# FFN gate and up computed as rows, with x stationary and the weights moving in four column groups, in a one-core decode kernel

## The chip, the cores and the metric

The kernel runs on one core of one Trainium2 chip. The metric is device time in microseconds (us), lower is better. Every time below is a median over executions of one program; the span in a profile is that of one profiled execution, some 1.5 us less than the device time. A change counts as faster or slower from 2% on. Experiments of one batch ran on one chip and share the runs of the kernel before.

Names: PE is TensorE (matmuls), PEld its weight loads, DVE is VectorE, ACT is ScalarE, SP is the engine whose queue issues the transfers. "K tile n" is the n-th of 32 tiles of the key cache, 8.4 MB each.

## The reference, cut to what matters

One decode step, batch 1, one token, D = 448. Part A is attention with 16 query heads over a cache of 8 heads x 65,536 positions x 256; part B is a small FFN; a gate mixes them. All inputs are bf16.

```python
gate = jnp.einsum("bsd,df->bsf", x, W_gate)      # W_gate, W_up: [448, 1792]
up   = jnp.einsum("bsd,df->bsf", x, W_up)
gate = gate * (gate > 0)
b    = jnp.einsum("bsf,fd->bsd", gate * up, W_down)
...
return g * a + (1 - g) * b                       # a: attention over the cache
```

The caches are 2 x 268.4 MB. The two FFN matrices that the change touches are 1.6 MB each.

## The kernel before

Three ring slots of 64 KB per partition take turns in holding tiles of K and V. At the start, slot 2 holds the weights of q, gate, up and down; K tile 0 goes to slot 0, K tile 1 to slot 1, and K tile 2 must wait until slot 2 is free. All these transfers are issued in order on one queue (SP). DVE transposes every K tile in eight pieces, PE multiplies it with q (QK), DVE takes the maximum, ACT the exponential.

The gate/up stage, before. F is 1792, R3 is 3, FT is 14. The *weights* are stationary, 128 columns at a time, and x moves, one column. So h comes out with its features on partitions, as the down projection wants it, but every matmul yields one column:

```python
def f_gu(e):
    for ft in range(FT):
        for which in range(2):                       # gate, up
            c = which * 14 + ft
            for kt in range(R3):
                e.matmul(GU_ps[:, c:c + 1], wf3[which][:, kt * F + ft:(kt + 1) * F:FT], xT[:, kt:kt + 1],
                         start=(kt == 0), stop=False, skip_group_check=True)
            for half in range(2):                    # the last 64 rows of D
                ins = e.matmul(GU_ps[64 * half:64 * half + 64, c:c + 1], wfh[which][:, ft:F // 2:FT],
                               xT[:, R3 + half:R3 + half + 1], start=False, stop=True, skip_group_check=True)
    return ins
```

An operation carries a key, and each engine runs its operations in the order of their keys. These keys matter here (`tk` and `tg` are planned landing times, 31.05 and 38.75):

```python
tr = [op("dv", tk + 2.22 * w, f_trans(sl, w), [kd]) for w in range(8)]   # transposes of a K tile
l_["relu"] = mop("dv", tg + 12, ...)                                     # 50.75: behind the transposes of K tile 0
l_["hT"]   = mop("dv", tg + 12.1, ...)
l_["dn"]   = op("pe", tg + 12.2, f_dn, [l_["hT"], a3])                   # 28 down matmuls; then slot 2 is free
qk[n, b]   = op("pe", tk + (9 * (b + 1) if n else 20 + b), ...)          # QK of tile 0 stands behind them
...
kd = dma("sp", t, "r%d" % sl, ..., free(("k", n)))                       # K tile 2: waits for gu and dn
```

Of the kernel before, what the change touches and what calls it, by code (L numbers as in the profile page):

```python
# [7 lines left out]
F32 = mybir.dt.float32  # L8
# [4 lines left out]
ALU = AluOpType  # L13
# [11 lines left out]
class _Plan:  # L25
# [8 lines left out]
    def op(self, eng, key, fn, deps=()):  # L34
        o = _Op(eng, key, fn, deps)
        self.ops.append(o)
        return o
# [82 lines left out]
def bass_gated_mix__gqa_block_cached__glu_gated_reglu__decode_kernel(  # L120
# [17 lines left out]
    F = B_W_gate.shape[1]  # L138
# [6 lines left out]
    R3 = D // 128  # L145
    NR3 = R3 * 128
    NX = R3 + 2
    FT = F // 128
# [7 lines left out]
    with es:  # L156
        sb = lambda name, shape, dt: es.enter_context(nc.sbuf_tensor(name, shape, dt))
# [3 lines left out]
        P_sb = sb("P_sb", [128, 2048], BF)  # L161
# [5 lines left out]
        identf = sb("identf", [128, 128], F32)  # L167
# [4 lines left out]
        xT = sb("xT", [128, NX], BF)  # L172
        gz = sb("gz", [1, 4], F32)
        gb = sb("gb", [128, 2], F32)
# [7 lines left out]
        X = sb("hs", [128, 20], F32)  # L182
        attnT = sb("attnT", [128, H * 4], BF)
        hT = sb("hT", [128, FT], BF)
        gtmp2 = sb("gtmp2", [128, FT], F32)


        xw = P_sb[:, 0:NX * 160]
        iot = P_sb[:, 800:1056].bitcast(I32)
        qn = P_sb[:, 1056:1568]  # L190
        x_row = P_sb[0:1, 2048 - D:2048]
        fin_o = P_sb[0:1, 0:D]
        gw_row = scr[0:1, 0:D]
# [7 lines left out]
        wf3 = [ring[2][:, WB + i * R3 * F:WB + (i + 1) * R3 * F] for i in range(2)]  # L201
        WB += 2 * R3 * F
        wfh = [ring[2][:, WB + i * (F // 2):WB + (i + 1) * (F // 2)] for i in range(2)]
# [5 lines left out]
        OP = ps("O", [128, 512], F32)  # L209
        A_ps = ps("A_ps", [128, 512], F32)  # L210
        M_ps = ps("M_ps", [128, 512], F32)
        QN_ps = ps("QN", [128, 512], F32)[:]
        VT_ps = M_ps[0:2, 0:128]
        NMR_ps = M_ps[:, 128:129]
        GU_ps = M_ps[:, 448:476]
        T_ps = M_ps[:, 480:484]
        GB_ps = M_ps[:, 496:498]
        LS_ps = M_ps[:, 500:502]
# [3 lines left out]
        op, dma = pl.op, pl.dma  # L222
        touch_m = []

        def mop(*a, **k):
            o = op(*a, **k)
            touch_m.append(o)
            return o
# [57 lines left out]
        c_ps = []  # L286
# [5 lines left out]
        g_idf = op("gp", 0.2, lambda e: e.tensor_scalar(identf[:], iot, 0.0, None, ALU.is_equal), [g_idb])  # L292
# [22 lines left out]
        z7 = mop("dv", 1.7, lambda e: e.tensor_copy(gb[:], GB_ps), [z6])  # L315
# [13 lines left out]
        x2_ = mop("dv", 0.7, lambda e: e.tensor_copy(xT[:], XT_ps), [x1_])  # L329
# [64 lines left out]
        l_, qk, smax, aexp, pv, last = {}, {}, {}, {}, {}, {}  # L394
# [55 lines left out]
        for kind, i, t in issue:  # L450
# [10 lines left out]
            elif kind == "gu":  # L461
                a1 = []
                for i_, W in enumerate((B_W_gate, B_W_up)):
# [2 lines left out]
                    a1.append(dma("sp", t + 0.01 * i_ + 0.005, "wfh%d" % i_, lambda e, W=W, i_=i_: e.dma_start(  # L466
                        wfh[i_], W[NR3:D, :].rearrange("r (t f) -> (r t) f", t=2))))

                def f_gu(e):
                    for ft in range(FT):  # L470
                        for which in range(2):
                            c = which * 14 + ft
                            for kt in range(R3):
                                e.matmul(GU_ps[:, c:c + 1], wf3[which][:, kt * F + ft:(kt + 1) * F:FT], xT[:, kt:kt + 1],  # L474
                                         start=(kt == 0), stop=False, skip_group_check=True)
                            for half in range(2):
                                ins = e.matmul(GU_ps[64 * half:64 * half + 64, c:c + 1], wfh[which][:, ft:F // 2:FT],  # L477
                                               xT[:, R3 + half:R3 + half + 1], start=False, stop=True, skip_group_check=True)
                    return ins
                tg = tL["gu", 0]  # L480
                l_["gu"] = mop("pe", tg, f_gu, a1 + [x2_])
                l_["relu"] = mop("dv", tg + 12, lambda e: e.tensor_scalar_max(gtmp2[:], GU_ps[:, 0:FT], 0.0), [l_["gu"]])
                l_["hT"] = mop("dv", tg + 12.1, lambda e: e.scalar_tensor_tensor(
                    hT[:], gtmp2[:], gb[:, 1:2], GU_ps[:, 14:14 + FT], ALU.mult, ALU.mult), [l_["relu"], z7])
            elif kind == "wd":
                a3 = dma("sp", t, "wd", lambda e: e.dma_start(wd_sb, B_W_down.rearrange("(p ft) d -> p ft d", ft=FT)), [l_["q"]])

# [6 lines left out]
            elif kind == "k":  # L494
                n = i
                h, t_ = divmod(n, NTH)
# [116 lines left out]
        pe = progs["pe"]  # L613
# [54 lines left out]
```

## Time and profile before

The kernel before takes 1277.39 us (6 runs, 1277.16 to 1277.75).

| | before |
|---|---|
| span of the profiled run | 1275.5 us |
| bytes read | 549.03 MB, 430 GB/s |
| busy PE / DVE / ACT | 33% / 50% / 5% |
| gate/up matmuls | 39.1 to 52.6 us |
| K tile 2 issued | 55.94 us |
| transposes of K tile 1 start | 63.22 us |

From the page of the kernel before: busy time by engine; the span in 40 equal slices, as tenths that the DMA engines were busy and as GB/s; the total.

```profile
PE 423.9 (33%) x4652; PEld 169.6 (13%) x4652; DVE 635.1 (50%) x428; ACT 63.4 (5%) x124; POOL 4.3 (0%) x21
...
DMA  9999999999999999999999999999999999999998
GB/s 402 447 427 428 434 434 442 432 430 432 436 436 436 430 432 432 434 438 436 427 432 438 436 432 434 432 432 432 438 438 427 432 436 436 434 434 432 419 442 351
...
HBM read 549.03 MB, written 0.00 MB: 430 GB/s over the span
...
L368 DVE STREAM_TRANSPOSE ring<-ring 128x2048 uint32<-128x2048 uint32 x256 | 565.4, 2275 | 395.2 <-DMA ring<-in_A_k_cache_dram 395.2
```

The last line says that DVE sat idle for 395.2 us before its transposes, waiting for DMA. No compute engine is near full. DMA is at its highest digit in every slice but the last and moves 419 to 447 GB/s in all but the first and the last.

The stage, from the timeline of the kernel before. Columns: start in us, duration in us (of a merged run of instructions, from the first start to the last end), engine, source line, operation, output<-inputs, shapes, count; in brackets the idle time before it and what ended that.

```profile
31.13 17.66 DVE L368 STREAM_TRANSPOSE ring<-ring 128x2048 uint32<-128x2048 uint32 x8 [7.77 <-DMA ring<-in_A_k_cache_dram]
39.11 0.31 PE L474 MATMUL M_ps<-xT,ring 128*128 128x1 bf16 x3 [17.58 <-DMA ring<-in_B_W_up_dram]
39.35 0.28 PE L477 MATMUL M_ps<-xT,ring 128*64 128x1 bf16 x2
...
52.64 0.17 DVE L482 TENSOR_SCALAR gtmp<-M_ps 128x14 f32<-128x14 f32 x1 [3.85 <-PE M_ps L477]
52.85 0.23 DVE L483 SCALAR_TENSOR_TENSOR hT<-gtmp,gb,M_ps 128x14 bf16<-128x14 f32 x1
53.13 2.40 PE L390 MATMUL A_ps<-ring,hT 128*1 128x224 bf16 x24 [0.53 <-DVE hT L483]
...
55.54 4.07 PE L379 MATMUL ST<-ring,xc 128*16 128x512 bf16 x62
55.94 4.05 SPq L498 DMA_DIRECT2D ring<-in_A_k_cache_dram  x2
...
63.22 2.31 DVE L368 STREAM_TRANSPOSE ring<-ring 128x2048 uint32<-128x2048 uint32 x1 [2.86 <-DMA ring<-in_A_k_cache_dram]
```

The last weights land at 39.1, PE works through the 140 matmuls, DVE makes hT, PE does the down matmuls, and at 55.94 the queue may issue K tile 2. At that moment K tile 1 is still on its way: DVE waits for it until 63.22. So the queue holds work when K tile 2 joins it. DVE spends 31.1 to 48.8 us in the transposes of K tile 0.

### The profile page before, as it was taken

The page shows a single profiled execution, that of the slowest core. Times are in us where ns is not written, and L with a number is a line of the kernel's source. Part 1 is how long each engine was busy: PE and PEld are TensorE (multiplying, and loading weights), DVE is VectorE, ACT ScalarE, POOL GpSimd, SP SyncE. Part 2 cuts the span into 40 slices and gives each one's busy share as a digit, 9 for nine tenths or more (in the row PEclk, how much of TensorE's full clock was granted, in tenths as well). Part 3 has the DMA queues.
Part 4 walks back from the last instruction along what each step waited for, and adds up shares of the span by engine and source line. Part 5 has one row for each costly group of instructions (what it writes and reads, how often), then busy time and mean ns, then how long its engine had stood idle before and what let it go on. Part 6 is the DMA issues. An engine that isn't in the chain of part 4 may idle for free. (4 is left out here: it accounts for less than half of the span.)

```text
span 1275.5 us, 10391 instructions
## 1 busy us (share of the span) xinstructions
PE 423.9 (33%) x4652; PEld 169.6 (13%) x4652; DVE 635.1 (50%) x428; ACT 63.4 (5%) x124; POOL 4.3 (0%) x21
## 2 busy tenths in 40 slices
PE   3633322334123532224331343321333314233235
PEld 1501110111001210011110111110111101011012
DVE  2597633465533655434555444555435655336600
ACT  0001000010000100001000010000100001000000
POOL 1000000000000000000000000000000000000000
PEclk8656666656666575667656666656666656666567
DMA  9999999999999999999999999999999999999998
GB/s 402 447 427 428 434 434 442 432 430 432 436 436 436 430 432 432 434 438 436 427 432 438 436 432 434 432 432 432 438 438 427 432 436 436 434 434 432 419 442 351
DMA packets 12052, 549.22 MB, mean 431 GB/s; under 512 B 1283, under 2 KB 1798, under 8 KB 3078
## 3 DMA queue, kind: packets, MB, share of 16 engines
q1 hardware_dynamic: 12034, 549.03, 99.7%
q8 instruction: 8, 0.13, 0.0%
q14 instruction: 6, 0.05, 0.0%
q10 hardware_dynamic: 4, 0.00, 0.0%
HBM read 549.03 MB, written 0.00 MB: 430 GB/s over the span
## 5 line engine op out<-in xcount | busy, mean ns | idle before, releaser
L368 DVE STREAM_TRANSPOSE ring<-ring 128x2048 uint32<-128x2048 uint32 x256 | 565.4, 2275 | 395.2 <-DMA ring<-in_A_k_cache_dram 395.2
L379 PE MATMUL ST<-ring,xc 128*16 128x512 bf16 x2048 | 222.1, 606 | 744.5 <-PEq L86 744.5
L379 PEld LDWEIGHTS ST<-ring,xc 128*16 128x16 bf16 x2048 | 67.9, 120 | 884.8 <-issue 883.8
L410 PE MATMUL O<-ring,ptp 128*4 128x512 bf16 x2048 | 147.7, 450 | 36.3 <-PEq L86 23.7
L509 ACT ACTIVATE P_sb<-ST,nmb 128x512 bf16<-128x512 f32 x32 | 45.3, 1415 | 1103.6 <-DVE nmb L507 1103.6
L507 DVE TENSOR_REDUCE nmb<-ST 128x1 f32<-128x512 f32 x32 | 22.0, 689 | 116.1 <-PE ST L379 116.1
L410 PEld LDWEIGHTS O<-ring,ptp 128*4 128x4 bf16 x2048 | 56.8, 99 | 126.7 <-issue 77.1
L420 DVE CAST o_sb<-O 128x512 bf16<-128x512 f32 x8 | 5.5, 691 | 76.1 <-PE O L410 76.1
L528 DVE TENSOR_TENSOR P_sb<-P_sb,hs 128x1024 bf16<-128x1024 bf16 x16 | 18.9, 1221 | 9.2 <-ACT hs L522 9.2
L533 PE MATMUL PT<-identb,P_sb 128*128 128x128 bf16 x128 | 16.2, 307 | 16.8 <-PEq L86 15.8
L474 PE MATMUL M_ps<-xT,ring 128*128 128x1 bf16 x84 | 9.5, 205 | 17.6 <-DMA ring<-in_B_W_up_dram 17.6
L533 PEld LDWEIGHTS PT<-identb,P_sb 128*128 128x128 bf16 x128 | 12.4, 138 | 19.2 <-issue 19.2
L542 ACT COPY ptp<-PT 128x256 bf16<-128x256 bf16 x32 | 10.3, 375 | 23.9 <-PE PT L533 23.9
L342 PE MATMUL QN<-ring,P_sb 128*128 128x512 bf16 x32 | 8.7, 439 | 3.9 <-DMA ring<-in_A_wq_dram 3.9
L474 PEld LDWEIGHTS M_ps<-xT,ring 128*128 128x128 bf16 x84 | 7.2, 151 | 18.2 <-issue 17.8
L509 ACT ACTIVATION_READ_ACCUMULATOR P_sb<-ST,nmb 128x1 f32 x32 | 8.5, 265 | 0.0
L477 PE MATMUL M_ps<-xT,ring 128*64 128x1 bf16 x56 | 7.8, 276 | 0.0
L457 DVE STREAM_TRANSPOSE scr<-P_sb 128x256 uint32<-128x256 uint32 x1 | 0.4, 445 | 13.1 <-ACT P_sb L456 13.1
L432 PE MATMUL M_ps<-emat,o_sb 128*64 128x1 bf16 x112 | 4.5, 199 | 6.6 <-PEq L86 6.6
L439 DVE TENSOR_SCALAR attnT<-M_ps,hs 64x4 bf16<-64x4 f32 x14 | 3.1, 220 | 6.3 <-PE M_ps L432 6.2
L518 PE MATMUL M_ps<-identf,hs 128*2 128x128 f32 x8 | 2.4, 295 | 11.1 <-PEq L86 11.1
L554 DVE RECIPROCAL hs<-M_ps 128x2 f32<-128x2 f32 x8 | 1.4, 170 | 8.3 <-PE M_ps L553 8.3
(77 smaller groups left out, 75.5 us busy)
## 6 DMA issues: line engine op xcount, KB each, us to landing
ring<-in_A_v_cache_dram SPq DMA_DIRECT2D x1, 4096.0 KB, 47.8
ring<-in_A_wq_dram SPq DMA_DIRECT2D x1, 3072.0 KB, 10.6
ring<-in_A_wo_dram SPq DMA_DIRECT2D x1, 2240.0 KB, 38.6
ring<-in_A_v_cache_dram SPq DMA_DIRECT2D x1, 2048.0 KB, 18.9
ring<-in_B_W_down_dram SPq DMA_DIRECT2D x1, 1568.0 KB, 22.1
ring<-in_B_W_gate_dram SPq DMA_DIRECT2D x1, 1344.0 KB, 32.3
ring<-in_B_W_up_dram SPq DMA_DIRECT2D x1, 1344.0 KB, 35.0
ring<-in_A_v_cache_dram SPq DMA_DIRECT2D x1, 1024.0 KB, 21.1
```

Of the source, the lines that this page charges most:

```text
L342: ins = e.matmul(QN_ps, xw3[:, k_, 31 - h:159 - h], rhs, start=(h == 0 and kt == 0), stop=(h == H - 1 and kt == R3))
L368: return lambda e: e.transpose(v, v)
L379: ins = e.matmul(bank[32 * w:32 * w + 16, :], xc[:, x0:x0 + 16], ktv[sl][:, u0:u0 + 16, c, :, r_], start=(b == 0 and c == 0 and r_ == 0), ...
L410: ins = e.matmul(OP[32 * g:32 * g + 4, :], ptp[:, col:col + 13:4], ring[sl][:, base + k * 512:base + (k + 1) * 512], start=(a == 0 and k < ...
L420: o1 = op("dv", tn, lambda e: e.tensor_copy(o_sb[:], OP[:]), [pv[n], last.get(("otr", h - 1))])
L474: e.matmul(GU_ps[:, c:c + 1], wf3[which][:, kt * F + ft:(kt + 1) * F:FT], xT[:, kt:kt + 1], start=(kt == 0), stop=False, skip_group_check= ...
L477: ins = e.matmul(GU_ps[64 * half:64 * half + 64, c:c + 1], wfh[which][:, ft:F // 2:FT], xT[:, R3 + half:R3 + half + 1], start=False, stop= ...
L507: smax[n] = op("dv", tk + 22, lambda e, n=n, NM=NM, t_=t_: e.tensor_reduce(NM[:, t_:t_ + 1], ST[n % 2][:], AX.X, ALU.max, negate=True), [q ...
L509: aexp[n] = op("ac", tk + 23, lambda e, n=n, t_=t_, NM=NM, RS=RS: e.activation(P_sb[:, t_:2048:4], ST[n % 2][:], ACTF.Exp, bias=NM[:, t_:t ...
L528: rsc = op("dv", tt, lambda e, X=X, pb=pb: e.tensor_tensor(pb, pb, X[:, 12:16].unsqueeze(1).to_broadcast([128, 256, 4]), ALU.mult), [h7, a ...
L533: ins = e.transpose(PT[rd][:, s * 128:(s + 1) * 128], P_sb[:, (rd * 8 + s) * 128:(rd * 8 + s + 1) * 128], identb[:, :])
L542: ins = e.copy(dst, src)
```

## The change

The intent is to swap the operands. x becomes stationary (one column), the weights move, 448 columns at a time, and four such matmuls lie side by side in four groups of 32 array columns. Gate and up then come out as rows, on partitions 0, 32, 64 and 96, in 32 matmuls. The price: the row h must be brought onto partitions again, by 14 small fp32 matmuls against an identity and four scalings.

```diff
-        GU_ps = M_ps[:, 448:476]
+        h_row = P_sb[:, 0:2 * F4].bitcast(F32)          # F4 = F // 4 = 448
+        HT_ps = M_ps[0:32, 256:256 + 4 * FT]
...
+                G_ps = (QN_ps, OP)
                 def f_gu(e):
-                    (loops over ft, which, kt and half: 140 matmuls, shown above)
+                    for which in range(2):
+                        for kt in range(R3 + 1):
+                            for g in range(4):
+                                lhs, rhs = (kt, wf3[which][:, kt * F + g * F4:kt * F + (g + 1) * F4]) if kt < R3 else \
+                                    (R3 + g // 2, wfh[which][:, g % 2 * F4:(g % 2 + 1) * F4])
+                                ins = e.matmul(G_ps[which][32 * g:32 * g + 1, 0:F4], xT[:, lhs:lhs + 1], rhs,
+                                               start=(kt == 0), stop=(kt == R3), skip_group_check=True, tile_position=(0, 32 * g))
+                    return ins
+                def f_hT(e):
+                    for ft in range(FT):
+                        ins = e.matmul(HT_ps[:, ft * 4:ft * 4 + 4], h_row[:, ft:F4:FT], identf[:, 0:128:32], start=True, stop=True)
+                    return ins
+                def f_hTc(e):
+                    for g in range(4):
+                        ins = e.tensor_scalar(hT[32 * g:32 * g + 32, :], HT_ps[:, g:4 * FT:4], gb[0:32, 1:2], None, ALU.mult)
                     return ins
...
-                l_["gu"] = mop("pe", tg, f_gu, a1 + [x2_])
+                l_["gu"] = op("pe", tg, f_gu, a1 + [x2_, l_["qn"], c_ps[2]])
-                l_["relu"] = mop("dv", tg + 12, lambda e: e.tensor_scalar_max(gtmp2[:], GU_ps[:, 0:FT], 0.0), [l_["gu"]])
-                l_["hT"] = mop("dv", tg + 12.1, ... scalar_tensor_tensor(hT, gtmp2, gb[:, 1:2], GU_ps[:, 14:14 + FT]) ...)
+                l_["relu"] = op("dv", tg + 12, lambda e: e.tensor_scalar_max(h_row, QN_ps[:, 0:F4], 0.0), [l_["gu"]])
+                l_["h"] = op("dv", tg + 12.05, lambda e: e.tensor_tensor(h_row, h_row, OP[:, 0:F4], ALU.mult), [l_["relu"]])
+                l_["hTp"] = mop("pe", tg + 12.1, f_hT, [l_["h"], g_idf])
+                l_["hT"] = mop("dv", tg + 12.15, f_hTc, [l_["hTp"], z7])
```

The keys of relu and of what follows it stay where they were, behind the transposes of K tile 0.

## The prediction

> **What bounds the kernel now.** The page moves 549 MB in a span of 1275.5 us, 430 GB/s. The row of slices shows DMA at 9 tenths in every slice but the last; in windows of 20 us from 120 to 1240 us it moves 426 to 446 GB/s, without a gap. The Trainium skill, "DMA: Bandwidth & Descriptors", section "Where 436 GB/s comes from", puts a core's fabric ceiling at 435 GB/s; this trace agrees. The engines have room: PE 33%, DVE 50%. The chain of waits runs through the last transfer and a tail of 2.8 us. So the time is bytes over rate plus that tail, and the change touches neither.
>
> **What the stage costs now.** Timeline: 140 gate/up matmuls from 39.1 (the last weights land) to 52.6 us, 96 ns each, at a granted clock of 0.5. Then two DVE operations (0.17 and 0.23), hT at 53.1, 28 down matmuls to 55.9, QK of tile 0 to 59.6 us. The freed FFN slot lets the queue issue K tile 2 at 55.94; slot 0 lets it issue K tile 3 at about 59.6.
>
> **What replaces it.** A QK group of 32 matmuls in the same four column groups, 512 columns, takes 3.59 us at the low clock (timeline at 72.3), so 448 columns give an estimate of 3.1 us: 39.1 to 42.3. But DVE runs in order and is inside the eight transposes of K tile 0, 31.13 to 48.8 us, and relu stands behind them: 6.5 us of the saving becomes a wait for DVE. Then relu and product on 128x448 fp32, about 0.65 us each (128x512 reduce 0.69; 448-column product 0.64): to about 50.2. The 14 fp32 transposing matmuls will show as 28, since plain fp32 matmuls show two instructions here; at an estimated 100 to 150 ns, 2.8 to 4.2 us: to about 53.6. Four 32x14 scalings at about 0.2 us: hT at about 54.5 (53 to 56): the old time or some 1.4 us later. PE busy falls by about 10 us, off the critical path.
>
> **How much is critical: none.** K tile 2 would be issued at about 57 us. K tile 1, ahead of it in the queue, lands only at about 62.9 (its transposes start at 63.2), so the queue still holds 5 to 6 us of work. K tile 3 has over 20 us of slack. Even if the stage took no time, DMA would gain nothing, because it is full already; the stage must slip by about 7 us before it opens a hole. DVE's maximum of tile 0 ends at about 62 and still fits before tile 1.
>
> **Predicted: 1277.3 us**, range 1275.0 to 1279.5. Faster by over 2%: 1%; within 2%: 98%; slower by over 2%: 1%.
>
> **What the profile would show.** Right: 32 matmuls of 448 columns in 3 to 3.5 us from 39.1; relu at about 48.9, after the transposes; 28 small fp32 matmuls in about 3 to 4 us; the down matmuls starting between 53 and 56; K tile 2 issued between 55 and 59; transposes of K tile 1 starting at 63.2 as before; DMA 9 in every slice, 430 GB/s; an unchanged chain at the end. Wrong: relu directly behind the row matmuls (then hT at about 47); a window near 60 to 66 us with low DMA share; K tile 2 issued after 62; or another tail.
>
> **What would make it wrong.** fp32 matmuls of over 300 ns, or a stall from changes of array tiling, adding over 5 us and starving the queue; each microsecond beyond the slack costs one, so even 10 us too many stay under 1%. A changed placement of instructions that disturbs the loop on PE would have to act in many tiles, for which I see no cause.

## The result

The changed kernel takes 1277.18 us (6 runs, 1277.11 to 1277.51) against 1277.39. The ratio is 0.9999, with a 95% interval from 0.9986 to 1.0012. Ratios here are the mean time of one kernel's fast runs over that of the other's of the same rounds, so not quite the ratio of the medians quoted. The output is correct.

From the page of the changed kernel, the lines that answer to those of the kernel before:

```profile
PE 423.0 (33%) x4572; PEld 162.0 (13%) x4572; DVE 636.7 (50%) x432; ACT 63.3 (5%) x124; POOL 4.3 (0%) x21
...
DMA  9999999999999999999999999999999999999998
...
HBM read 549.03 MB, written 0.00 MB: 430 GB/s over the span
...
L369 DVE STREAM_TRANSPOSE ring<-ring 128x2048 uint32<-128x2048 uint32 x256 | 565.4, 2275 | 390.0 <-DMA ring<-in_A_k_cache_dram 390.0
```

And the stage in the timeline of the changed kernel:

```profile
31.17 17.66 DVE L369 STREAM_TRANSPOSE ring<-ring 128x2048 uint32<-128x2048 uint32 x8 [6.52 <-DMA ring<-in_A_k_cache_dram]
38.96 1.66 PE L478 MATMUL QN<-ring,xT 128*1 128x448 bf16 x16 [16.14 <-DMA ring<-in_B_W_up_dram]
...
40.41 1.50 PE L478 MATMUL O<-ring,xT 128*1 128x448 bf16 x16
...
48.76 0.58 DVE L493 TENSOR_SCALAR P_sb<-QN 128x448 f32<-128x448 f32 x1
49.38 0.62 DVE L494 TENSOR_TENSOR P_sb<-P_sb,O 128x448 f32<-128x448 f32 x1
...
50.05 1.94 PE L484 MATMUL M_ps<-identf,P_sb 128*32 128x4 f32 x28 [8.14 <-DVE P_sb L494]
52.03 0.93 DVE L489 TENSOR_SCALAR hT<-M_ps,gb 32x14 bf16<-32x14 f32 x4 [2.03 <-PE M_ps L484]
...
53.01 2.40 PE L391 MATMUL A_ps<-ring,hT 128*1 128x224 bf16 x24 [1.03 <-DVE hT L489]
...
55.42 5.34 PE L380 MATMUL ST<-ring,xc 128*16 128x512 bf16 x62
55.83 5.32 SPq L510 DMA_DIRECT2D ring<-in_A_k_cache_dram  x2
...
63.18 4.50 DVE L369 STREAM_TRANSPOSE ring<-ring 128x2048 uint32<-128x2048 uint32 x2 [1.67 <-DMA ring<-in_A_k_cache_dram]
```

The matmuls did what they were meant to: gate and up take 2.95 us (38.96 to 41.91) in place of 13.5. But PE is then idle for 8.14 us. Relu has no bracket: DVE comes to it straight from the last transpose, not from waiting for PE. The row operations, the transposing matmuls and the scalings fill 48.76 to 52.96, and the down matmuls start at 53.01 in place of 53.13. K tile 2 is issued at 55.83 in place of 55.94. The transposes of K tile 1 start where they did.

So there are two separate reasons why the gain is invisible: the stage as a whole ends where it ended, and, by the theory, its end would not matter anyway. The experiments take them apart.

### The profile page after: what moved, and what is told of

The parts are those of the page before. It is cut to its first block, busy times and chain, and to the rows that moved or that the text cites. A ratio compares the mean times of both kernels' runs of the same rounds, so it can differ in the third digit from the quotient of the medians.

```text
span 1275.7 us, 10235 instructions
## 1 busy us (share of the span) xinstructions
PE 423.0 (33%) x4572; PEld 162.0 (13%) x4572; DVE 636.7 (50%) x432; ACT 63.3 (5%) x124; POOL 4.3 (0%) x21
## 5 line engine op out<-in xcount | busy, mean ns | idle before, releaser
L380 PE MATMUL ST<-ring,xc 128*16 128x512 bf16 x2048 | 225.2, 613 | 738.4 <-PEq L86 738.4
L411 PE MATMUL O<-ring,ptp 128*4 128x512 bf16 x2048 | 150.5, 457 | 36.6 <-PEq L86 24.4
L433 PEld LDWEIGHTS M_ps<-emat,o_sb 128*64 128x64 bf16 x112 | 4.1, 154 | 9.9 <-issue 9.9
L532 PE MATMUL M_ps<-mx,nselT 2*128 2x1 f32 x16 | 3.6, 292 | 4.1 <-PEq L86 4.1
```

The source lines that it names most:

```text
L380: ins = e.matmul(bank[32 * w:32 * w + 16, :], xc[:, x0:x0 + 16], ktv[sl][:, u0:u0 + 16, c, :, r_], start=(b == 0 and c == 0 and r_ == 0), ...
L411: ins = e.matmul(OP[32 * g:32 * g + 4, :], ptp[:, col:col + 13:4], ring[sl][:, base + k * 512:base + (k + 1) * 512], start=(a == 0 and k < ...
L433: ins = e.matmul(T_ps[64 * q:64 * q + 64, s:s + 1], o_sb[:, par * 256 + s:par * 256 + 256:4], emat[:, 2 * par + q:2 * par + q + 1], start= ...
L532: h5 = mop("pe", T + 15, lambda e, h=h: e.matmul(NMR_ps, nselT[0:2, :], mx2[0:2, 0:1], start=True, stop=True), [h4, l_["ns"]])
```

## The experiments

**Theory.** The time is bytes over DMA rate plus a short tail. The stage has slack: it may end at any time before the queue runs dry behind K tile 1.

**Rivals.** (1) The stage *is* critical, and the gain was merely eaten by the wait for DVE; then freeing relu should pay. (2) DMA only looks full, and the loop on PE and DVE sets the pace; then fewer bytes should not pay. (3) A hole in the queue at the start is made up later, so that nothing in the stage could ever matter.

The kernels of e1 to e6 are edits of the changed kernel; e7 and e8 are the two kernels themselves. Batch 1 (e1, e2, e3, e6): the kernel before took 1277.35 us in 9 runs. Batch 2 (e4, e5, e7, e8): 1277.27 us in 7 runs.

### e1: relu in between the transposes

```diff
-l_["relu"] = op("dv", tg + 12, ...)        +l_["relu"] = op("dv", tg + 3.2, ...)
-l_["h"]    = op("dv", tg + 12.05, ...)     +l_["h"]    = op("dv", tg + 3.25, ...)
-l_["hTp"]  = mop("pe", tg + 12.1, ...)     +l_["hTp"]  = mop("pe", tg + 3.5, ...)
-l_["hT"]   = mop("dv", tg + 12.15, ...)    +l_["hT"]   = mop("dv", tg + 3.6, ...)
-l_["dn"]   = op("pe", tg + 12.2, ...)      +l_["dn"]   = op("pe", tg + 3.7, ...)
```

> The changed kernel with relu, product and scaling moved up in DVE's program order, so that they stand between the transposes of K tile 0 and not behind them. Theory (DMA is full and the stage has slack): relu starts at about 42.3 us, hT is ready near 47.5 in place of 53.0, K tile 2 is issued near 50 in place of 55.8, and the time stays at 1277.2, within 0.6 us. Rival (the stage is on the critical path, and the change gained nothing only because relu waits for the transposes): the time falls by about 5 us.

Measured: 1277.10 us (5 runs, 1277.05 to 1277.37), ratio 0.9998 (0.9984 to 1.0011). From its timeline:

```profile
42.25 0.62 DVE L493 TENSOR_SCALAR P_sb<-QN 128x448 f32<-128x448 f32 x1
...
46.61 2.40 PE L391 MATMUL A_ps<-ring,hT 128*1 128x224 bf16 x24 [1.10 <-DVE hT L489]
...
49.42 4.82 SPq L510 DMA_DIRECT2D ring<-in_A_k_cache_dram  x2
...
63.33 17.66 DVE L369 STREAM_TRANSPOSE ring<-ring 128x2048 uint32<-128x2048 uint32 x8 [8.72 <-DMA ring<-in_A_k_cache_dram]
```

Relu now starts as soon as the rows are done, and the down matmuls start 6.4 us earlier than in the changed kernel (46.61 against 53.01). K tile 2 is issued 6.4 us earlier, too. And nothing happens: DVE still waits for K tile 1 until 63.33, now for 8.72 us. The time saved was turned into a longer wait for DMA. This shows that the order on DVE was what held the stage's end, and that the stage's end is not critical. Rival 1 falls.

### e2: the same, and rows and transposes in bf16

```diff
(the keys of e1; hTp waits for g_idb in place of g_idf)
-h_row = P_sb[:, 0:2 * F4].bitcast(F32)
+h_row = P_sb[:, 0:F4]
-    ... h_row[:, ft:F4:FT], identf[:, 0:128:32] ...
+    ... h_row[:, ft:F4:FT], identb[:, 0:128:32] ...
```

> As the run before, and relu, product and the 14 transposing matmuls in bf16: 14 PE instructions in place of 28. Theory: the transposing matmuls take about 1 us in place of 1.94, hT is ready near 46.5, still right within tolerance, and the time stays at 1277.2 within 0.6 us. Rival (stage critical): 6 us faster.

Measured: 1277.17 us (5 runs, 1277.07 to 1277.32), ratio 0.9998 (0.9985 to 1.0012), correct. The transposing matmuls took 1.00 us in place of 1.94. But hT was ready at 46.23, not much before e1's 46.56: the scalings stand behind a transpose piece on DVE in both (45.34 here, 45.67 in e1), so most of that microsecond became a wait as well. The time did not move, as the theory expects.

### e3, e4, e5: making the stage longer

The transposing matmuls are done 3, 7 and 13 times over, to the same values. This leaves the result right and delays the release of slot 2 by a known amount. What follows on PE and DVE moves with it, the issue of K tile 3 too; so we look for the hole directly before K tile 2.

```diff
-for ft in range(FT):
+for ft in list(range(FT)) * 3:      # 7 in e4, 13 in e5
     ins = e.matmul(HT_ps[:, ft * 4:ft * 4 + 4], h_row[:, ft:F4:FT], identf[:, 0:128:32], start=True, stop=True)
```

> The changed kernel with the 14 transposing matmuls done three times over (same values). The stage ends 3.9 us later, and K tile 2 is issued near 59.7. Theory (about 7 us of slack before K tile 1 has drained): no change, within 0.6 us of 1277.2. Rival (stage critical): about 3.9 us slower, 1281.

> The changed kernel with the transposing matmuls seven times over: the stage ends 11.6 us later and K tile 2 is issued near 67.5, after K tile 1 has landed (about 62.9). Theory: the queue runs dry for about 5.5 us (4.5 to 7.5), seen as a stretch of low DMA share near 62 to 68, and the time rises by as much, to about 1282.7. Rival A (stage critical from the start): 11.6 us slower, 1288.8. Rival B (later slack absorbs a hole): no change.

> The same thirteen times over: the stage ends 23.3 us later, K tile 2 is issued near 79. Theory: slope one beyond the slack, so about 11.6 us more than with seven times: about 17 us (16 to 19) over 1277.2, so near 1294.3. Rival A: 23.3 us slower, 1300.5. Rival B: under 10 us slower.

| kernel | K tile 2 issued, us | time, us (runs) | over the kernel before of its batch |
|---|---|---|---|
| e1 | 49.42 | 1277.10 (1277.05 to 1277.37) | -0.25 |
| changed kernel | 55.83 | 1277.18 (1277.11 to 1277.51) | -0.21 |
| e3, 3 times | 59.14 | 1277.55 (1277.14 to 1279.61) | +0.20 |
| e4, 7 times | 66.48 | 1283.01 (1282.88 to 1283.42) | +5.74 |
| e5, 13 times | 77.02 | 1293.85 (1293.68 to 1294.3) | +16.58 |

The issues of K tile 2, one line each from the timelines of e3, e4 and e5:

```profile
59.14 0.33 SPq L510 DMA_DIRECT2D ring<-in_A_k_cache_dram  x1
66.48 0.33 SPq L510 DMA_DIRECT2D ring<-in_A_k_cache_dram  x1
77.02 0.33 SPq L510 DMA_DIRECT2D ring<-in_A_k_cache_dram  x1
```

From the view of stretches, first of the changed kernel, then of e4, then of e5. Columns: the stretch in us, its length; busy us and count of PE, PEld, DVE, ACT, POOL; the granted PE clock; the DMA share; GB/s. (A DMA packet counts in the stretch in which it starts, so shares in short stretches swing and can pass 1; only large differences count.)

```profile
60.00:66.00 6.00, 0.77 (x14) 0.13 (x4) 3.51 (x3) 1.39 (x2) 0.00 (x0) 0.95 1.13 483
66.00:76.00 10.00, 2.46 (x24) 0.89 (x28) 10.00 (x5) 0.00 (x0) 0.00 (x0) 0.50 0.99 428
```

```profile
60.00:66.00 6.00, 4.98 (x70) 4.21 (x73) 0.89 (x4) 0.00 (x0) 0.00 (x0) 0.50 0.04 15
66.00:76.00 10.00, 4.79 (x70) 3.18 (x60) 5.15 (x4) 1.40 (x2) 0.00 (x0) 0.84 0.98 401
```

```profile
60.00:66.00 6.00, 6.00 (x98) 6.00 (x97) 0.00 (x0) 0.00 (x0) 0.00 (x0) 0.50 0.04 14
66.00:76.00 10.00, 8.97 (x134) 8.35 (x135) 0.89 (x4) 0.00 (x0) 0.00 (x0) 0.50 0.01 2
```

Here is the hole: 15 GB/s over 60 to 66 us in e4 where the changed kernel has 483, and 14 and 2 GB/s over 60 to 76 in e5. From e4 to e5 the issue moves by 10.54 us (77.02 - 66.48) and the time by 10.84 (16.58 - 5.74), a slope of 1.03. Both losses lie in the expected ranges. Nearly all of the time lost in this place stays lost, and rival 3 falls. Taking the slope as one, the loss of e4 reaches back to an issue at 60.7 us (66.48 - 5.74) and that of e5 to 60.4 (77.02 - 16.58). So the changed kernel has a slack of about 4.7 us (60.5 - 55.83). This is an estimate from two runs and a straight line.

The DMA packets in the kept traces show why the slack ends there. In e4 and e5 the 16 DMA engines finish K tile 1 one after another: the first at 60.8 to 60.9 us, 15 of them by 61.7, the last at 62.9 to 63.0. After the issue of K tile 2 they start on it 0.95 to 2.25 us later. So most engines run dry unless the issue comes well before K tile 1 has landed. Counted so, an engine has no packet for 6.4 us in e4 and 17.1 us in e5 (means of the 16). This is 0.5 to 0.7 us more than the time lost, so no more than that was made up.

e3, issued 59.14, lies just within the straight-line estimate. Three of its five runs took 1277.14 to 1277.55, and two took 1279.06 and 1279.61. So it does not hold to "no change" in every execution; the edge is not sharp to a microsecond. The profiled run is one of the two (1279.06). In its trace one of the 16 engines has no packet from 61.0 to 62.5 us, and DVE gets its later K tiles 1.0 us behind the kernel before (103.02 against 102.06). So half of this loss began here. The other half came far from the stage: the lag is 2.0 us from 452.34 us on (against 450.37). What caused that half was not tried, and the other slow run has no profile.

### e6: fewer bytes, all the compute

```diff
-for i_, W in enumerate((B_W_gate, B_W_up)):
+for i_, W in enumerate((B_W_gate,)):
-    ... wf3[which] ... wfh[which] ...
+    ... wf3[0] ... wfh[0] ...
```

> The changed kernel without the load of the up weights (1.57 MB of 549.03 MB); the gate weights are used twice, so the result is wrong on purpose. Every compute instruction stays. Theory (bytes over rate): 1.61 million bytes at 433 GB/s are 3.7 us, so about 1273.5 us. Rival (the loop on PE and DVE sets the pace, and DMA only looks full because its queue is kept filled): no change, 1277.

Measured: 1274.04 us (5 runs; four of them 1273.57 to 1274.36, one 1276.02), ratio 0.9978 (0.9964 to 0.9991). The result is wrong. All the instructions of PE, DVE and ACT remain. The medians differ by 3.3 us, where 3.7 were expected; the interval excludes "no change" and holds the expected ratio (1 - 3.7/1277.35 = 0.9971). Its stage ended at the same time as that of the changed kernel (K tile 2 issued at 55.91). So leaving out 0.3% of the bytes pays, while taking 6.4 us off the stage (e1) does not. Alone, this does not exclude rival 2: the missing bytes stand ahead of K tile 1, so a loop that waits for that tile at its start would have started earlier too. The profiles close this gap. In the kernel before, DVE waits for DMA at the start of each of the 32 K tiles, 395.2 us in all, and in the kept traces of all ten runs each of the 16 DMA engines has a packet at practically every moment from 80 to 1240 us. Rival 2 falls: DMA sets the pace.

### e7 and e8: both kernels again, for the clock

In the first pair of profiles, 62 of the QK matmuls of tile 0 took 4.07 us before and 5.34 after. This costs nothing here, but it looked like a side effect of the pause of PE that the change opens.

> The kernel before, unchanged, for a second profile. Question: in the first pair of profiles the QK matmuls of tile 0 took 4.07 us before and 5.34 after, at a granted clock of 0.99 and 0.67 over 56 to 60 us. If the PE pause that the change opens (42 to 50 us) is the cause, each kernel repeats its own figure within 0.3 us; if it is chance in when the clock is raised, the two figures vary from run to run by a microsecond or more.

> The changed kernel, unchanged, for a second profile, with the same question: QK of tile 0 again at 5.3 us (the pause is the cause) or anywhere between 4 and 6.5 us (chance). Time 1277.2 within 0.6 us.

Measured: both kernels took 1277.11 us (one run each). QK of tile 0 took 4.43 us in the kernel before and 5.28 in the changed one. In e6, which has the same pause, it was 5.00; in e1 and e2, 4.84 and 4.59; in e3, e4 and e5, where PE works for 5.5, 12.6 and 23.2 us on transposing matmuls between the pause and the down matmuls, 4.18, 4.71 and 4.01. By the clock records of the traces, the granted clock goes from 0.5 to 1.0 between 2.7 and 5.6 us after the first down matmul over these ten profiles.

Neither expectation came out clean. The kernel before moved by 0.36 us between its profiles, the changed one by 0.06, and the two groups did not overlap. The Trainium skill, "TensorE: Matmul & The Clock Gate", section "What's actually happening", says that the clock is raised after one busy window of about 3.4 us and that the window is free-running. The ten traces agree on the second point: within a profile, all changes of the granted clock lie whole multiples of 3.413 us apart (in the changed kernel, for example, at 41.56, 44.98 and 58.63 us), and where these periods fall differs from profile to profile.

The rise at QK follows from this. It comes at the end of the first period of which the down and QK matmuls fill 2.7 us or more (2.71 in e5, 2.91 in e3, 2.93 in the first profile of the kernel before). A period of which they fill 2.2 us or less is passed over (2.20 and 1.92 in the two profiles of the changed kernel, 1.46 in e6, 1.09 in e1). This reading fits all ten profiles without the pause of PE, so the figures are best explained by chance in where the periods fall. It stays a reading: no run shifted the periods on purpose.

## Why the prediction was right

A forecast of "no change" would come out right under several theories. It is the experiments, not the time alone, that bear out its reason.

- **The bound.** "The time is bytes over rate plus that tail, and the change touches neither": shown. e6 took bytes away and gained 3.3 us; e1 took time out of the stage and gained nothing. The rate was 430 GB/s over the span in both kernels, and DVE waited for DMA at every K tile.
- **"6.5 us of the saving becomes a wait for DVE"**: the row matmuls ended at 41.91 and relu started at 48.76, 6.85 us. e1 shows that it was DVE's program order. The Trainium skill, "TensorE: Matmul & The Clock Gate", section "Architectural detail: the array is 16× 32×32, not 1× 128×128", calls DVE strict FIFO; this trace agrees, since relu starts at the end of the eighth transpose.
- **The row matmuls**, "an estimate of 3.1 us": 2.95. Relu and product, "about 0.65 us each": 0.58 and 0.62. Scalings "at about 0.2": 0.22 each.
- **The fp32 transposing matmuls** were over-costed. Twenty-eight instructions was right, "an estimated 100 to 150 ns" was not: 1.94 us / 28 = 69 ns each. So hT came at 52.96, just outside the "53 to 56" given, and the stage ended 0.1 us earlier than before, not 1.4 later.
- **"The stage must slip by about 7 us before it opens a hole"** was the step mis-sized most. The lines through e4 and e5 put it at about 4.7 us. The prediction took the moment at which K tile 1 is *seen* to have landed (63.2) as the moment until which the next transfer may be issued; the runs put that moment 2.7 us earlier (60.5). K tile 1 landed as forecast (62.9, also in e4), but 15 of 16 DMA engines had finished with it by 61.7, and none started on K tile 2 sooner than 0.95 us after its issue. The text's other figure, "5 to 6 us of work", took off the issue at 57 but made the same mistake.
- **"PE busy falls by about 10 us"**: within 39.1 to 53.0 us it fell from 13.49 to 4.75, 8.7 us. On the page it fell only from 423.9 to 423.0, because PE's total differs by several microseconds between profiles of one kernel (423.9 and 427.3 before, 423.0 and 418.3 after): a difference of that size is not to be read from the total.
- **"An unchanged chain at the end"**: in both profiles the chain of waits ends with the last transfer and then 3.2 us of PE and DVE, 1271.11 to 1274.31 before and 1271.33 to 1274.53 after. (The prediction wrote 2.8 for this tail, which is PE's part alone; it cancels in the comparison.)
- **No version beat both kernels.** The shortest stage tried (e2) takes the same time. What is left to gain is in bytes, and the reference fixes these.

## What to carry to other kernels

Ask first whether a stage's end is on the critical path: find the transfer that its end releases, and how much work the queue still holds at that moment. When DMA is full, the matmuls of a stage can become four times faster and the kernel not at all; make the stage longer by steps and you learn how much slack it has, and that it counts one for one beyond it. And when the producer gets faster, look at where its consumer stands in the order of its own engine.

## What the Trainium skill lacked or had wrong

- "DMA: Bandwidth & Descriptors" gives a first-byte latency for this path (about 0.6 us) but not how early the next transfer must be issued to leave no gap behind the one before. Here a loss began with an issue about 2.7 us before DVE could start on the earlier transfer (60.5 against 63.2), and with an issue at 59.14 (e3), about 4 us before that moment, two of five runs still lost about 2 us. The engines finished the earlier transfer over 2 us (60.8 to 62.9) and started on the next 0.95 to 2.25 us after its issue (e4, e5).
- "TensorE: Matmul & The Clock Gate" says that about 3.4 us of sustained activity raises the clock. Here 140 one-column matmuls kept PE busy for 13.49 of 13.50 us at a granted clock of 0.50, and so did the 364 fp32 instructions of e5 over 23.2 us. Busy in the trace is not what the clock counts; the page exempts only transposes. Nor does it say how full a window must be: of the down and QK matmuls, 2.71 us in one period were enough (e5) and 2.20 us were not (the changed kernel).
- The same page, in what it says of small matmuls, does not say what a small fp32 matmul costs in a stream. Here each plain fp32 matmul shows as two instructions; with 32 stationary and 4 moving columns they took 69 ns each (28 in 1.94 us), and in bf16 71 ns each (14 in 1.00 us, e2): here the cost went by the instruction, and fp32 had two.
